# Two token tiles of the last second-layer chunk as float32r matmuls

## The chip, the cores and the metric

The kernel runs on one core of a Trainium2 chip. The metric is the device time of one execution in microseconds. A core has five engines that run side by side and meet by semaphores: TensorE (PE, matmuls; its weight loads are shown apart as PEld), VectorE (DVE), ScalarE (ACT), GpSimd (POOL) and SyncE (SP, which here only starts transfers).

## The reference

```python
# q, k, v: (8, 8, 576, 64) float32; heads 0-3 see the last 32 positions, heads 4-7 every 32nd
scores = where(mask, q @ k.T / 8, -1e9)
attn = softmax(scores)
x = (attn @ v).transpose(0, 2, 1, 3).reshape(4608, 512)
# w_in: (512, 2048), w_out: (2048, 512)
h = x @ w_in
r = maximum(h, 0)
g = r * r
out = g @ w_out                       # (4608, 512) float32
```

It is a sparse attention over 8 batches and 8 heads, followed by two dense layers with a squared ReLU between them, over 4608 tokens.

## The kernel before

Attention writes its result, transposed and in bf16, into four tiles `xt` of 128 channels by 4608 tokens. The dense layers work through nine chunks of 512 tokens. In each chunk the first layer (`mm1`) goes through 16 blocks of 128 hidden units: four matmuls of 512 columns each, from `w_in_b` and `xt`, into one of TensorE's accumulation banks; ScalarE takes the ReLU into a small bf16 tile `r` (four buffers); and one step later (`later(1, ...)`) VectorE multiplies `r` by itself into block `ff` of `g_sb`, a tile of 128 by 16 by 512 in bf16. The second layer (`mm2`) then takes the chunk as four tiles of 128 tokens. For each, 16 matmuls of 512 columns add up over the hidden blocks, with a piece of `g_sb` as the weights and a row of `w_out_b` as the moving operand; ScalarE copies the bank to `y`, and SyncE stores it.

```python
for ff in range(4 * part, 4 * part + 4):
    nc.tensor.matmul(py, g[:, ff, 128 * j:128 * (j + 1)], w_out_b[:, ff, :],
                     start=(ff == 0), stop=(ff == 15))
```

The last tile of the last chunk (`last_y`) is split by columns into 256, 128 and 128, so that its last copy and store are small.

All this stands in one list, `groups`: 288 entries, 16 for the first and 16 for the second layer of each chunk. The last chunk's first layer is entries 256 to 271, its second layer 272 to 287, four entries for each token tile. A hand-written table, `PLAN`, says ahead of which entry each step of attention is issued (loads, transposes, scores, normalisations); the last is at entry 217. Each engine carries out its own instructions in the order in which they are issued (`manual_schedule`), and waits are set where one engine's data is needed by another. So the list and the table set the order.

Memory: most tiles live in the pool `singles` for the whole kernel, and the tiles of attention in this and some further pools (`qk_in`, `qkT`, `v_st`, `rv_pool`, `xl_pool`, `strTq`, `strTk`), all open until the end.

Of the kernel before, what the change touches and what calls it, by code (L numbers as in the profile page):

```python
# [8 lines left out]
FP32 = mybir.dt.float32  # L9
BF16 = mybir.dt.bfloat16  # L10
AF = mybir.ActivationFunctionType
ALU = mybir.AluOpType
# [155 lines left out]
def kernel(  # L168
# [9 lines left out]
    nc = tc.nc  # L178
    B, H, S, D = q.shape
# [6 lines left out]
    NL = S // QL  # L186
# [4 lines left out]
    VP = 72  # L191
    SR = 80
    NP2 = STRIDE // 2
    NG = 5
    NB = NP2 + NG + 1
    W3 = 3 * NA
    RW = STRIDE * D
    ER = S + 32

    singles = ctx.enter_context(tc.tile_pool(name="singles", bufs=1))  # L200
    qk_in = ctx.enter_context(tc.tile_pool(name="qk_in", bufs=4))
    qkT = ctx.enter_context(tc.tile_pool(name="qkT", bufs=4))
    v_st = ctx.enter_context(tc.tile_pool(name="v_st", bufs=1))
    rv_pool = ctx.enter_context(tc.tile_pool(name="rv_pool", bufs=3))
    small = ctx.enter_context(tc.tile_pool(name="small", bufs=4))
    xl_pool = ctx.enter_context(tc.tile_pool(name="xl_pool", bufs=4))
    g_pool = ctx.enter_context(tc.tile_pool(name="g_pool", bufs=2))
    r_pool = ctx.enter_context(tc.tile_pool(name="r_pool", bufs=4))
    y_pool = ctx.enter_context(tc.tile_pool(name="y_pool", bufs=4))

    PS = bass.MemoryType.PSUM
    strTs = {nm: ctx.enter_context(tc.tile_pool(name=f"strT{nm}", bufs=n)) for nm, n in (("q", 2), ("k", 1))}
    psum = ctx.enter_context(tc.tile_pool(name="psum", bufs=1, space=PS))
    psb = psum.tile([128, 8, 512], FP32, name="psb")
    all_banks = [psb[:, i] for i in range(8)]
# [4 lines left out]
    def bank(nm):  # L220
        if places:
            return all_banks[places.pop(0)]
        t = banks[nm].pop(0)
        banks[nm].append(t)
        while id(t) in unread:
            run_due(lambda x: x[1] == unread[id(t)])
        return t
# [10 lines left out]
    NV = 4  # L238
# [1 line left out]
    mask_loc = singles.tile([128, 1, QL], BF16)  # L240
    mask_all = singles.tile([128, NL, QL], BF16)
    mask_str = singles.tile([SP_, 1, SP_], BF16)
    vl_all = singles.tile([128, NV, 2, NL, VP], BF16, name="vl")
    vls = [vl_all[:, i] for i in range(NV)]

    vbds = [singles.tile([128, NB, 128], BF16, name=f"vb{i}") for i in range(2)]
    kbds = [singles.tile([128, NB, 128], BF16, name=f"kb{i}") for i in range(2)]
    ones_bd = singles.tile([128, 128], BF16)
    mask_bd = singles.tile([128, 1, W3], BF16)
    str_rows_t = {nm: singles.tile([SR, RW], BF16, name=f"{nm}_t") for nm in "qk"}  # L250
    kTl = [singles.tile([128, 32 + S], BF16, name=f"kTl{i}") for i in range(NV)]
    es01 = singles.tile([128, 4 * ER], BF16, name="e01")
    es = [es01[:, 0:2 * ER], es01[:, 2 * ER:]] + [singles.tile([128, 2 * ER], BF16, name=f"e{i}") for i in (2, 3)]
    xt = [singles.tile([128, T], BF16, name=f"xt{p}") for p in range(4)]
    w_in_b = singles.tile([128, 4, d_ff], BF16)
    w_out_b = singles.tile([128, 16, d_model], BF16)
# [210 lines left out]
    def later(n, fn, key=None):  # L467
        pending.append((clock[0] + n, key, fn))

    def run_due(test):  # L470
        due = [x for x in pending if test(x)]
        for x in due:
            pending.remove(x)
        for x in sorted(due, key=lambda x: x[0]):
            x[2]()

    def tick():
        clock[0] += 1
        run_due(lambda x: x[0] <= clock[0])
# [247 lines left out]
    gs = {}  # L727
# [3 lines left out]
    def mm1(c, ff, kks=range(4), order=range(4), pool=None):  # L731
        if ff == 0 and c not in gs:
            gs[c] = g_pool.tile([128, 16, 512], BF16, name="g_sb")
        g = gs[c]
        if kks[0] == order[0]:
            phs[ff] = bank(pool or "ph")
        ph = phs[ff]
        for kk in kks:
            nc.tensor.matmul(ph, w_in_b[:, kk, 128 * ff:128 * (ff + 1)],  # L739
                             xt[kk][:, 512 * c:512 * (c + 1)],  # L740
                             start=(kk == order[0]), stop=(kk == order[-1]))
        if kks[-1] != order[-1]:
            return
        r = r_pool.tile([128, 512], BF16, name="r")
        nc.scalar.activation(r, ph, AF.Relu)  # L745
        later(1, lambda: nc.vector.tensor_tensor(g[:, ff, :], r, r, op=ALU.mult))  # L746
# [3 lines left out]
    def mm2(c, i, pool=None):  # L750
        j, part = divmod(i, 4)
        g = gs[c]
        if part == 0:
            if pool == "pt":
                ys[c, j] = bank("pt")
                banks["pt"].remove(ys[c, j])
            else:
                ys[c, j] = bank(pool or "py")
        py = ys[c, j]
# [3 lines that stand above are left out]
        if part == 3:  # L763
            y = y_pool.tile([128, 512], FP32, name="y")
            nc.scalar.copy(y, py)  # L765
            if pool == "pt":
                banks["pt"].insert(0, py)
            r0 = 512 * c + 128 * j
            nc.sync.dma_start(out=out[r0:r0 + 128, :], in_=y)

    NCH = T // 512
# [3 lines left out]
    def last_y(c, j, i):  # L775
        g, r0 = gs[c], 512 * c + 128 * j
        if i == 0:
            ys[c, j] = y_pool.tile([128, 512], FP32, name="y")
        y = ys[c, j]
        cols = (slice(0, 256), slice(0, 256), slice(256, 384), slice(384, 512))[i]  # L780
        ffs = (range(0, 8), range(8, 16), range(16), range(16))[i]
        if i != 1:
            ys[c, j, i] = bank("ph")
        py = ys[c, j, 0 if i == 1 else i]
        for ff in ffs:
            nc.tensor.matmul(py[:, cols], g[:, ff, 128 * j:128 * (j + 1)], w_out_b[:, ff, cols],  # L786
                             start=(ff == 0), stop=(ff == 15))
        if i:
            (V if i == 3 else A)(y[:, cols], py[:, cols])
            (nc.scalar if i == 2 else nc.sync).dma_start(out=out[r0:r0 + 128, cols], in_=y[:, cols])  # L790
# [156 lines left out]
    groups = []  # L947

    def add(c, kind, i, pool=None):
        if kind == 0:  # L950
            groups.append(lambda: None)
        elif kind == 1:
            groups.append(lambda: mm1(c, i, pool=pool))
        elif c == NCH - 1 and i >= 12:
            groups.append(lambda: last_y(c, i // 4, i % 4))
        else:
            groups.append(lambda: mm2(c, i, pool))

    for ff in range(16):
        add(0, 1, ff, {NP: "pt", 8: "py"}.get(ff)) if ff >= NP else add(0, 0, ff)  # L960
    for part in range(4):
        for j, pool in ((0, "ph"), (1, "ph"), (2, None), (3, "pt")):
            add(0, 2, 4 * j + part, pool)
    for i in range(16):
        add(1, 1, i)
# [9 lines left out]
    for line in PLAN.strip().splitlines():  # L975
        n, words = line.split(":")
        plan.setdefault(int(n), []).extend(words.split())
    for n, g in enumerate(groups):
        if n == 32:
            banks["pt"] += banks.pop("py")  # L980
        for word in plan.get(n, ()):
            run_step(word)
        g()
        tick()
# [32 lines left out]
```

## Time and profile before

| | |
|---|---|
| median of two timed runs | 298.03 us (297.99 and 298.07) |
| the profiled execution | 299.14 us |
| its span, first to last instruction | 297.4 us |
| granted TensorE clock | 1.00 |
| PE busy | 287.8 us, 97% of the span |
| DVE busy | 180.3 us, 61% |
| ACT busy | 170.5 us, 57% |
| POOL busy | 73.3 us, 25% |
| first-layer matmuls (L739) on the longest chain | 42% of the span |
| second-layer matmuls (L761) on it | 40% |

The profile is of one execution, whose own time is the 299.14 us; the span leaves out what lies before its first and after its last instruction. Matmuls overlap in the pipeline, so the length recorded for one (379 ns for 512 columns) is more than the distance from one start to the next. A row of a group of instructions gives line, engine, operation, operands, shape and count, then busy time in us and mean length in ns, then the engine's idle time just ahead of them and what ended it. A row of a timeline or of the chain begins with its start and its length in us; several equal instructions in a row are merged there into one with their count.

### The profile page before, as it was taken

To read this page: it belongs to the slowest core of one execution; us is meant where nothing else is said; L and a number is where in the kernel's file an instruction comes from. 1 tells how busy PE (TensorE), PEld (TensorE's weight loads), DVE (VectorE), ACT (ScalarE), POOL (GpSimd) and SP (SyncE) were. 2 spreads that over 40 slices of the span, in tenths; PEclk is the share of its full clock that TensorE was granted. 3 is DMA by queue.
4 is the path that set the end of the run, shared out by engine and by line. 5 is a ranking of instruction groups with operands and counts; after the bars stand their busy time and mean duration, and the time that the engine had idled before them with its cause. 6 is when DMAs were issued, how large, how long until landed. Compare 5 with 4: busy or idle time off the path is not lost.

```text
span 297.4 us, 5621 instructions
## 1 busy us (share of the span) xinstructions
PE 287.8 (97%) x2112; PEld 144.6 (49%) x2148; DVE 180.3 (61%) x465; ACT 170.5 (57%) x318; POOL 73.3 (25%) x107
## 2 busy tenths in 40 slices
PE   7989999999999999999999999999999999999994
PEld 2644555544545454444454445544544444444444
DVE  5557689697777769779367936776575334004300
ACT  3758846774668636764577447744764266127411
POOL 8874743014513036065105700000000000000000
PEclk9999999999999999999999999999999999999999
DMA  7999999999999999999998999411011100020012
GB/s 146 183 207 204 189 199 189 156 224 204 168 179 179 123 164 199 160 144 188 179 128 125 177 149 145 82 55 73 35 31 47 71 37 0 35 89 20 0 71 73
DMA packets 91724, 37.38 MB, mean 126 GB/s; under 512 B 77549, under 2 KB 85831, under 8 KB 91697
## 3 DMA queue, kind: packets, MB, share of 16 engines
q0 software_dynamic: 50608, 18.33, 55.8%
q1 hardware_dynamic: 40944, 18.62, 32.3%
q8 instruction: 17, 0.28, 0.4%
q14 instruction: 11, 0.08, 0.1%
q10 hardware_dynamic: 144, 0.07, 0.1%
HBM read 37.22 MB, written 9.44 MB: 157 GB/s over the span
## 4 chain that ended last, share of the span: by engine, by line
PE 94%; DMA 2%; issue 1%; DVE 1%; ACT 0%; POOL 0%; DVEq 0%; POOLq 0%
PE psb L739 42%; PE psb L761 40%; DMA w_out_b<-in_k_dram 2%; PE psb L699 2%; PE psb L621 1%; PE psb L607 1%; PE psb L786 1%; PE psb L618 1%; PE psb L583 1%; PE psb L538 1%; PE psb L486 1%; DVE xt L668 0%; PE psb L508 0%; PE psb L333 0%; DVE x_l L688 0%
## 5 line engine op out<-in xcount | busy, mean ns | idle before, releaser
L739 PE MATMUL psb<-xt,w_in_b 128*128 128x512 bf16 x558 | 132.1, 379 | 1.2 <-DVE xt L668 0.2
L761 PE MATMUL psb<-w_out_b,g_sb 128*128 128x512 bf16 x542 | 125.3, 379 | 1.2 <-issue 0.5
L745 ACT ACTIVATE r<-psb 128x512 bf16<-128x512 f32 x144 | 85.3, 599 | 37.9 <-PE psb L739 32.8
L746 DVE TENSOR_TENSOR g_sb<-r 128x512 bf16<-128x512 bf16 x144 | 60.4, 423 | 68.5 <-ACT r L745 67.2
L739 PEld LDWEIGHTS <-w_in_b 128*128 128x128 bf16 x576 | 53.2, 97 | 58.9 <-issue 1.4
L761 PEld LDWEIGHTS <-g_sb 128*128 128x128 bf16 x560 | 52.0, 98 | 57.9 <-DVE g_sb L746 0.3
L765 ACT COPY y<-psb 128x512 f32<-128x512 f32 x35 | 20.6, 588 | 51.6 <-PE psb L761 48.6
L631 DVE TENSOR_TENSOR xt<-psb,rv 64x144 bf16<-64x144 f32 x84 | 34.0, 405 | 12.7 <-ACT rv L624 11.6
L623 ACT ACTIVATE rv<-psb 128x432 f32<-128x432 f32 (+1 forms) x21 | 10.5, 501 | 12.8 <-PE psb L618 12.8
L705 DVE TENSOR_TENSOR x_l<-psb,rinv 96x384 bf16<-96x384 f32 x28 | 15.5, 553 | 1.0
L361 POOL DMA_DIRECT2D q_t<-in_q_dram x6 | 3.3, 544 | 45.8 <-DMA qT_s<-q_t 44.9
L594 ACT ACTIVATE e<-psb 128x384 bf16<-128x384 f32 x30 | 12.0, 513 | 4.2 <-PE psb L583 4.2
L608 ACT ACTIVATE e<-psb 128x432 bf16<-128x432 f32 (+1 forms) x21 | 10.4, 496 | 4.0 <-PE psb L607 4.0
L637 DVE TENSOR_TENSOR xt<-psb,rv 64x270 bf16<-64x270 f32 (+1 forms) x28 | 11.0, 433 | 2.5 <-ACT rv L624 2.3
L290 POOL DMA_DIRECT2D q_l<-in_q_dram x16 | 12.0, 754 | 1.6 <-DMA q_l<-in_q_dram 1.4
L290 POOL DMA_DIRECT2D k_l<-in_k_dram x16 | 11.7, 736 | 1.6 <-DMA v_st<-in_v_dram 1.5
L624 ACT ACTIVATE rv<-rv 128x432 f32<-128x432 f32 (+1 forms) x21 | 11.2, 533 | 0.7
L590 DVE TENSOR_TENSOR e<-e,mask_all 128x576 bf16<-128x576 bf16 x20 | 8.4, 456 | 4.9 <-ACT e L594 4.9
L699 PEld LDWEIGHTS <-e 128*128 128x128 bf16 x168 | 8.0, 97 | 4.6
L361 POOL DMA_DIRECT2D k_t<-in_k_dram x6 | 3.2, 536 | 25.0 <-DMA kT_s<-k_t 22.9
L699 PE MATMUL psb<-vl,e 128*128 128x65 bf16 x168 | 9.0, 193 | 0.0
L607 PEld LDWEIGHTS <-kb 128*128 128x128 bf16 x154 | 6.8, 96 | 4.5
(119 smaller groups left out, 213.5 us busy)
## 6 DMA issues: line engine op xcount, KB each, us to landing
out_dram<-y SPq DMA_DIRECT2D x35, 256.0 KB, 4.2
w_out_b<-in_moe_w_out_dram POOLq DMA_DIRECT2D x4, 512.0 KB, 15.1
q_t<-in_q_dram POOLq DMA_DIRECT2D x7, 288.0 KB, 7.3
k_t<-in_k_dram POOLq DMA_DIRECT2D x7, 288.0 KB, 6.9
vl<-in_v_dram POOLq DMA_DIRECT2D x6, 288.0 KB, 7.7
v_st<-in_v_dram POOLq DMA_DIRECT2D x7, 216.0 KB, 6.8
w_in_b<-in_moe_w_in_dram POOLq DMA_DIRECT2D x2, 704.0 KB, 14.3
k_l<-in_k_dram POOLq DMA_DIRECT2D x16, 72.0 KB, 7.0
```

The lines of the kernel that those rows point to most:

```text
L290: nc.gpsimd.dma_start(out=t[:, :, hh, :], in_=src[b, 2 * p + hh].rearrange("(t p) d -> p t d", p=QL))
L594: nc.scalar.activation(e[:, row, 4 * QL * i:4 * QL * (i + 1)], bk[row][i][:, 0:4 * QL], AF.Exp, scale=scale)
L624: nc.scalar.activation(rv, rv, AF.Exp, scale=-1.0)
L631: nc.vector.tensor_tensor(to[:, :, NJ * part:NJ * (part + 1), par], of, by, op=ALU.mult)
L637: nc.vector.tensor_tensor(t, of[:, g:, :, lo:lo + k], by[:, g:, :, lo:lo + k], op=ALU.mult)
L699: nc.tensor.matmul(po[:, n, :], e[:, c:c + 128], rhs[:, NL * part + n, 0:D + 1], start=True, stop=True)
L705: nc.vector.tensor_tensor(x, po[0:QL, :, 0:D], rinv[0:QL].to_broadcast([QL, NL, D]), op=ALU.mult)
L739: nc.tensor.matmul(ph, w_in_b[:, kk, 128 * ff:128 * (ff + 1)], xt[kk][:, 512 * c:512 * (c + 1)], start=(kk == order[0]), stop=(kk == order ...
L745: nc.scalar.activation(r, ph, AF.Relu)
L746: later(1, lambda: nc.vector.tensor_tensor(g[:, ff, :], r, r, op=ALU.mult))
L761: nc.tensor.matmul(py, g[:, ff, 128 * j:128 * (j + 1)], w_out_b[:, ff, :], start=(ff == 0), stop=(ff == 15))
L765: nc.scalar.copy(y, py)
```

## The change

The pools that only attention uses, and the attention tiles out of `singles` (now in `att_singles`), are put on a stack of their own, `att`. Ahead of entry 230, after the last step of attention has been issued, this stack is closed, and a pool `late` is opened in the freed memory. It holds a float32r copy of the whole of `w_out_b`, a small tile of zeros in bf16, and for each of two token tiles a float32r copy of its part of `g_sb`.

- `widen`, ahead of entries 230, 232, ... 244: the first call sets the zeros on VectorE; each of the eight calls has GpSimd copy two of the 16 rows of `w_out_b` (1024 elements per partition) into the float32r tile.
- `mm2_r(0)` at entry 272 and `mm2_r(1)` at entry 276 stand in for token tiles 0 and 1 of the last chunk. Each first makes its float32r copy of g: blocks 0 to 7 by a copy, blocks 8 to 15 by a sum with the zeros, on VectorE for tile 0 and on GpSimd for tile 1. Then tile 0 runs 16 matmuls of 512 columns, and tile 1 runs 16 matmuls for the left 256 columns and 16 for the right, all with float32r operands. ScalarE's copy to `y` and the store follow as before.
- A float32r matmul stands in the order as one instruction that brings its own weights, where a bf16 one is a weight load and a matmul. So TensorE has 48 instructions in place of 64 there; all others, on all engines, keep their order. VectorE has three instructions more, GpSimd ten.

The rest of the last chunk (tiles 2 and 3) and all other chunks stay as they are.

```diff
-    qk_in = ctx.enter_context(tc.tile_pool(name="qk_in", bufs=4))
...
+    att = ctx.enter_context(ExitStack())
+    att_singles = att.enter_context(tc.tile_pool(name="att_singles", bufs=1))
+    qk_in = att.enter_context(tc.tile_pool(name="qk_in", bufs=4))
...
-    vl_all = singles.tile([128, NV, 2, NL, VP], BF16, name="vl")
+    vl_all = att_singles.tile([128, NV, 2, NL, VP], BF16, name="vl")
...
+        elif c == NCH - 1 and i < 8:
+            groups.append((lambda: mm2_r(i // 4)) if i % 4 == 0 else (lambda: None))
...
+    F32R = mybir.dt.float32r
+    wide = {}
+
+    def widen(i):
+        if not wide:
+            att.close()
+            late = ctx.enter_context(tc.tile_pool(name="late", bufs=1))
+            wide["w"] = late.tile([128, 16, 512], F32R, name="w_out_r")
+            wide["z"] = late.tile([128, 8, 128], BF16, name="zeros")
+            nc.vector.memset(wide["z"], 0.0)
+            wide["g"] = [late.tile([128, 16, 128], F32R, name=f"g_r{j}") for j in range(2)]
+        nc.gpsimd.tensor_copy(wide["w"][:, i:i+2, :].rearrange("p a c -> p (a c)"), w_out_b[:, i:i+2, :].rearrange("p a c -> p (a c)"))
+
+    def mm2_r(j):
+        c = NCH - 1
+        r0 = 512 * c + 128 * j
+        y = y_pool.tile([128, 512], FP32, name="y")
+        py = bank("ph")
+        gr, w = wide["g"][j], wide["w"]
+        eng = nc.vector if j == 0 else nc.gpsimd
+        g = gs[c][:, :, 128 * j:128 * (j + 1)]
+        eng.tensor_copy(gr[:, 0:8], g[:, 0:8])
+        eng.tensor_tensor(gr[:, 8:16], g[:, 8:16], wide["z"], op=ALU.add)
+        for lo, hi in ((0, 512),) if j == 0 else ((0, 256), (256, 512)):
+            for ff in range(16):
+                nc.tensor.matmul(py[:, lo:hi], gr[:, ff, :], w[:, ff, lo:hi], start=ff == 0, stop=ff == 15)
+        nc.scalar.copy(y, py)
+        nc.sync.dma_start(out=out[r0:r0 + 128, :], in_=y)
+
     for n, g in enumerate(groups):
+        if 230 <= n < 246 and n % 2 == 0:
+            widen(n - 230)
```

More of the change, by code (lines that the diff above doesn't have):

```diff
@@ L200 @@
     singles = ctx.enter_context(tc.tile_pool(name="singles", bufs=1))
-    qk_in = ctx.enter_context(tc.tile_pool(name="qk_in", bufs=4))
-    qkT = ctx.enter_context(tc.tile_pool(name="qkT", bufs=4))
-    v_st = ctx.enter_context(tc.tile_pool(name="v_st", bufs=1))
-    rv_pool = ctx.enter_context(tc.tile_pool(name="rv_pool", bufs=3))
     small = ctx.enter_context(tc.tile_pool(name="small", bufs=4))
-    xl_pool = ctx.enter_context(tc.tile_pool(name="xl_pool", bufs=4))
     g_pool = ctx.enter_context(tc.tile_pool(name="g_pool", bufs=2))
@@ L209 @@
     y_pool = ctx.enter_context(tc.tile_pool(name="y_pool", bufs=4))
+    att = ctx.enter_context(ExitStack())
+    att_singles = att.enter_context(tc.tile_pool(name="att_singles", bufs=1))
+    qk_in = att.enter_context(tc.tile_pool(name="qk_in", bufs=4))
+    qkT = att.enter_context(tc.tile_pool(name="qkT", bufs=4))
+    v_st = att.enter_context(tc.tile_pool(name="v_st", bufs=1))
+    rv_pool = att.enter_context(tc.tile_pool(name="rv_pool", bufs=3))
+    xl_pool = att.enter_context(tc.tile_pool(name="xl_pool", bufs=4))
     PS = bass.MemoryType.PSUM
-    strTs = {nm: ctx.enter_context(tc.tile_pool(name=f"strT{nm}", bufs=n)) for nm, n in (("q", 2), ("k", 1))}
+    strTs = {nm: att.enter_context(tc.tile_pool(name=f"strT{nm}", bufs=n)) for nm, n in (("q", 2), ("k", 1))}
     psum = ctx.enter_context(tc.tile_pool(name="psum", bufs=1, space=PS))
@@ L242 @@
     mask_str = singles.tile([SP_, 1, SP_], BF16)
-    vl_all = singles.tile([128, NV, 2, NL, VP], BF16, name="vl")
+    vl_all = att_singles.tile([128, NV, 2, NL, VP], BF16, name="vl")
     vls = [vl_all[:, i] for i in range(NV)]
-    vbds = [singles.tile([128, NB, 128], BF16, name=f"vb{i}") for i in range(2)]
-    kbds = [singles.tile([128, NB, 128], BF16, name=f"kb{i}") for i in range(2)]
+    vbds = [att_singles.tile([128, NB, 128], BF16, name=f"vb{i}") for i in range(2)]
+    kbds = [att_singles.tile([128, NB, 128], BF16, name=f"kb{i}") for i in range(2)]
     ones_bd = singles.tile([128, 128], BF16)
     mask_bd = singles.tile([128, 1, W3], BF16)
[L250 to L253, printed above, removed]
+    str_rows_t = {nm: att_singles.tile([SR, RW], BF16, name=f"{nm}_t") for nm in "qk"}
+    kTl = [att_singles.tile([128, 32 + S], BF16, name=f"kTl{i}") for i in range(NV)]
+    es01 = att_singles.tile([128, 4 * ER], BF16, name="e01")
+    es = [es01[:, 0:2 * ER], es01[:, 2 * ER:]] + [att_singles.tile([128, 2 * ER], BF16, name=f"e{i}") for i in (2, 3)]
     xt = [singles.tile([128, T], BF16, name=f"xt{p}") for p in range(4)]
```

## The prediction

> **What bounds the kernel now.** I read the page first, then the chain of waits, then the timeline of the stretch in which the changed tiles run. The page, its lines on the span, the engines' busy time, the clock and the chain:
>
> ```profile
> span 297.4 us, 5621 instructions
> PE 287.8 (97%) x2112; PEld 144.6 (49%) x2148; DVE 180.3 (61%) x465; ACT 170.5 (57%) x318; POOL 73.3 (25%) x107
> PEclk9999999999999999999999999999999999999999
> PE 94%; DMA 2%; issue 1%; DVE 1%; ACT 0%; POOL 0%; DVEq 0%; POOLq 0%
> ```
>
> TensorE is the bound: 97% busy, at full clock in all 40 slices, and 94% of the chain. So a microsecond added to TensorE, or a microsecond in which it has to wait, is a microsecond of the kernel. The changed work lies in the last 18 us. The chain of waits there, in order of time (start, length, what):
>
> ```profile
> 270.44 9.23 PE psb L739 x42
> 279.67 1.51 PE psb L761 x7
> 281.18 0.05 issue
> 281.23 8.80 PE psb L761 x40
> 290.03 3.55 PE psb L786 x48
> 293.57 0.04 DVEq L789
> 293.61 0.04 issue
> 293.65 0.29 DVE y L789
> ```
>
> First-layer matmuls of the last chunk (L739) run to 279.67, and the second layer (L761, then the split last tile, L786) follows without a gap. The only hops are 0.04 to 0.05 us. How that gaplessness comes about shows in the timeline at the seam (start, length, engine, line, operation):
>
> ```profile
> 277.13 2.54 PE L739 MATMUL psb<-xt,w_in_b 128*128 128x512 bf16 x11
> 279.47 0.42 DVE L746 TENSOR_TENSOR g_sb<-r 128x512 bf16<-128x512 bf16 x1 [0.44 <-ACT r L745]
> 279.50 5.34 PE L761 MATMUL psb<-w_out_b,g_sb 128*128 128x512 bf16 x23
> 279.70 0.60 ACT L745 ACTIVATE r<-psb 128x512 bf16<-128x512 f32 x1 [0.27 <-PE psb L739]
> 280.33 0.42 DVE L746 TENSOR_TENSOR g_sb<-r 128x512 bf16<-128x512 bf16 x1 [0.44 <-ACT r L745]
> ```
>
> The second layer starts at 279.50, while the last block of g is finished only at 280.33 + 0.42 = 280.75. That costs nothing now, because the blocks are used in order: the 16th matmul of the tile, the one that reads that block, comes 15 matmuls later. This lead is what the change spends. The pace of the matmuls: 11 of them take 2.54 us with 0.38 of that the last one's own length, so 2.16 / 10 = 0.216 us from start to start at 512 columns. For narrower ones:
>
> ```profile
> 289.86 3.70 PE L786 MATMUL psb<-w_out_b,g_sb 128*128 128x256 bf16 x48
> L786 PE MATMUL psb<-w_out_b,g_sb x48: 218/219/273, 289.9 to 293.3; 128*128 128x128 bf16 x32, 128*128 128x256 bf16 x16
> L786 PEld LDWEIGHTS <-g_sb x48: 97/98/98, 289.6 to 293.3; 128*128 128x128 bf16 x48
> ```
>
> 16 of 256 columns and 32 of 128 start within 3.70 - 0.22 = 3.48 us. Counted in units of 128 columns that is 63 steps, 0.055 us each: 0.055 us at 128 columns, 0.11 at 256. Each brings its own weight load, recorded at 98 ns, yet the pace goes down to 55 ns: bf16 weight loads lie wholly under other matmuls.
>
> **The change, part by part.**
>
> *A. Tile 0 gets a wait in front.* Its 16 matmuls read a float32r copy of g. VectorE makes it in two instructions of 1024 elements per partition: a copy (blocks 0 to 7), then a sum with zeros (blocks 8 to 15). In the built order both stand on VectorE behind all 16 squares of the chunk, although the copy needs only the first eight. So the copy cannot start before 280.75. Its price is not in the trace; the nearest rows (mean ns is the number after the busy time):
>
> ```profile
> L309 DVE CAST k_l<-g_sb 96x768 bf16<-96x768 f32 x1 | 0.6, 557 | 0.1
> L430 DVE COPY vb<-v_st 54x1408 bf16<-54x1408 bf16 x14 | 7.4, 531 | 0.5 <-DMA v_st<-in_v_dram 0.3
> L688 DVE TENSOR_TENSOR x_l<-psb,rinv 96x768 bf16<-96x768 f32 x2 | 1.9, 954 | 0.1
> L705 DVE TENSOR_TENSOR x_l<-psb,rinv 96x384 bf16<-96x384 f32 x28 | 15.5, 553 | 1.0
> ```
>
> Below, the all-bf16 copy, 531 x 1024 / 1408 = 0.39 us. Above, the rate at which a float32 operand is worked through one element at a time: (954 - 553) / 384 = 1.04 ns, so 954 + 256 x 1.04 = 1.22 us. The nearest is the cast L309, the other way round but also between float32 and bf16 in SBUF: twice as fast as 1.04, so 557 + 256 x 0.52 = 0.69 us. I take 0.69. TensorE's first float32r matmul waits for nine semaphores, carried by four extra wait instructions; the others have long been reached, and one of the four stands behind the copy's:
>
> ```profile
> L739 PEldq EVENT_SEMAPHORE  x1: 51/51/51, 113.4 to 113.4; - x1
> ```
>
> So it starts at 280.75 + 0.03 + 0.69 + 0.05 (hop, as in the chain) + 0.05 = 281.57 instead of 279.50: **+2.07 us**, with the ends of the copy +1.8 and +2.6. Behind this wait in TensorE's queue stands all that is left of the kernel, and the stores wait for that; nothing can fill the gap, as tiles 2 and 3, which need no copies, come later in the order.
>
> *B. The second half of tile 0.* The sum is priced at the upper rate, 1.22 us, since both operands and the result pass one by one: done at 281.47 + 1.22 = 282.69. Its first reader is the ninth matmul, 281.57 + 8 x 0.216 = 283.30. **0**, covered by 0.6 us. If a GpSimd instruction held VectorE up there, this cover is gone (a rival, below).
>
> *C. Tile 0's matmuls.* 16 x 0.216 before. The trace has no float32r matmul. Low end: the same pace, 0. High end: the weight load, which is now part of the matmul, no longer slips under the one before: 98 ns each, 16 x 0.098 = +1.6. A 512-column matmul leaves 216 ns to hide a load that fits into 55 in bf16; even with twice the bytes it should. I take **0**.
>
> *D. Tile 1 as 32 matmuls of 256 columns.* 32 x 0.108 = 16 x 0.216, so the split costs nothing by columns. But there are now 32 weight loads instead of 16, and 108 ns to hide each. Low end 0.108; if a load of twice the bytes takes 98 + 55 = 0.153 us and only the next can run ahead, the pace is 0.153; if nothing is hidden, 0.108 + 0.098 = 0.206 (+3.1 us). I take the middle of the first two, 0.130: 32 x 0.022 = **+0.7**.
>
> *E. Tile 1's copies on GpSimd.* The copy waits for the eighth square, the sum for the last. The rows for it:
>
> ```profile
> 273.43 0.43 DVE L746 TENSOR_TENSOR g_sb<-r 128x512 bf16<-128x512 bf16 x1 [0.44 <-ACT r L745]
> ```
>
> ```profile
> 169.59 0.62 POOL L426 DMA_DIRECT2D v_st<-in_v_dram  x1
> ```
>
> ```profile
> L898 POOL MEMSET kb<- 128x1408 f32 x2 | 2.6, 1291 | 0.0
> masks.py:199 POOL TENSOR_SCALAR_AFFINE_SELECT ident<-ident 128x128 bf16<-128x128 bf16 x1 | 0.3, 287 | 0.1
> ```
>
> GpSimd is idle from 170.2 on. 1024 elements cost it between 0.94 us (the memset's 0.917 ns) and 2.3 us (the short select's 2.24 ns, fixed cost included). The copy runs from 273.86 and is done by 276.2. The sum runs from 280.8; even behind both of VectorE's instructions it ends at 282.69 + 2.3 = 285.0. Tile 1 begins at 281.57 + 3.45 = 285.02, and the ninth matmul, the first reader, at 285.9. **0**, covered by 0.9 us.
>
> *F. The eight copies of w_out on GpSimd, and the zeros on VectorE.* 8 x 0.94 to 8 x 2.3 = 7.5 to 18.4 us. They wait for the last users of the freed memory:
>
> ```profile
> 217.88 4.81 SPq L714 DMA_TRANSPOSE xt<-x_l  x2
> 233.04 1.57 DVE L637 TENSOR_TENSOR xt<-psb,rv 64x270 bf16<-64x270 f32 x4 [1.13 <-ACT rv L624]
> 239.76 0.43 DVE L746 TENSOR_TENSOR g_sb<-r 128x512 bf16<-128x512 bf16 x1 [5.14 <-ACT r L745]
> L905 DVE MEMSET xt<- 128x256 uint32 x1 | 0.3, 272 | 0.9 <-PEq L1001 0.9
> ```
>
> All of that is over at 234.6, so they end by 253.0, 28 us ahead of their reader. Nothing stands behind them on GpSimd but tile 1's copies, 20 us later. The zeros take about 2 x 0.27 = 0.54 us among squares that have 0.44 us idle before each, with four r buffers between them and ScalarE: a delay of 0.1 us that the next square makes good. **0** each. The pools that are moved change no instruction's place and no wait before these.
>
> *Sum.* 2.07 + 0 + 0 + 0.7 + 0 + 0 = +2.8 us. The profiled execution, 299.14 us with a span of 297.4, would become 301.9; the median of the two runs, 298.03, lies 1.1 lower, and I forecast there: **300.8 us**.
>
> **The rivals.**
>
> *1. Weight loads in series: slower.* Speaks for it: the load is part of the matmul and has no place of its own in the order, so that it may not be pulled ahead. Against: in bf16 nearly half of a 128-column step's load record lies under other work. Price: 1.6 + 3.1 + 2.07 = +6.8, 304.8 us. With +2.07 from A, it crosses 2% (+5.96) once 48 matmuls lose 81 ns each. Chance 0.14.
>
> *2. A 4-byte stream at half rate: slower.* The weight load is hidden, but each row brings twice the bytes: 0.431 us at 512 columns, 0.216 at 256, so twice 3.45 us more: 2.07 + 6.9 = +9.0, 307.0 us. For it: no 4-byte operand of TensorE is in this trace, so nothing shows that its read has bytes to spare. Against: with 128 columns a weight load and a moving read go on side by side every 55 ns, so in bf16 its reads are not at their end. Chance 0.08. The Trainium skill, SBUF, section "A bandwidth-pool intuition that's wrong (but worth ruling out)", gives TensorE's moving read as about 614 GB/s, written out as 2 bytes per lane and cycle; held to that, this rival would come true. No row here shows it. The skill's FP8 and Floating Point Precision, section "TensorE Precision Notes", speaks the other way: it describes a reduced mode that reads 4-byte values and truncates them, beside a true float32 of four passes.
>
> *3. The change is no reduced mode: four passes, as for float32: slower.* 3 x 6.9 = 20.7 more, +22.8, 320.8 us. Chance 0.05.
>
> *4. The sum on GpSimd goes ahead of VectorE's.* Both become ready while VectorE's copy runs. If GpSimd's gets hold of what they share at 281.47, VectorE's sum ends at 281.47 + 2.3 + 1.22 = 284.99, and the ninth matmul waits 1.7 us: 302.5 us, within 2%. For it: both start within 0.7 us of each other on the same tiles. Against: VectorE's is next in its own queue. Chance 0.06. The skill's SBUF, section "SBUF: two separate sides", calls the port pair of the two engines an exclusive lock that the first one holds for its whole instruction; no instruction of GpSimd that reads SBUF meets VectorE late in this trace, so it cannot say.
>
> *5. Faster.* There is no step that shortens TensorE's work, only 48 issues in place of 64, and issue is 1% of the chain. Chance 0.01.
>
> **How the numbers follow.** The forecast (A with one pass and nearly hidden loads) 0.66, rival 4 0.06, rival 1 0.14, rival 2 0.08, rival 3 0.05, faster 0.01. Slower by over 2%, about what a measurement of this kernel can tell from no change: 0.14 + 0.08 + 0.05 = 0.27; within 2%: 0.72; faster: 0.01. Range: the low end is the short copy and no loss in D, 298.03 + 1.8 = 299.8, less a little for noise; the high end takes in rival 1, 304.9. Left outside: rivals 2 and 3 and 0.03 more.
>
> **What would show it.** In the chain after: a piece of VectorE (the copy) of 0.4 to 1.2 us between the last square and the first float32r matmul, and a gap of about 2.1 us on TensorE between the layers. Starts of tile 0's matmuls 0.216 us apart, of tile 1's 0.108 to 0.153; 0.3 apart is rival 1, 0.43 rival 2, 0.86 rival 3. No wait at the ninth matmul of either tile. The w_out copies over before 253. The forecast is wrong if the gap is under 1.7 or over 2.7 us, or if the two tiles together take over 8.3 us.

## The result and the profile after

The changed kernel takes 302.21 us (median of two runs, 301.97 and 302.44) against 298.03 us before (297.99 and 298.07): a ratio of 1.014, 95% interval 1.0096 to 1.0184. It is 4.2 us slower, by less than 2%. The forecast was 300.8 us.

The profiled execution took 301.97 us. Three of the four lines of its page that were shown of before (the page's own chain breaks off at 283.92, so its shares do not compare):

```profile
span 300.1 us, 5680 instructions
PE 288.9 (96%) x2128; PEld 148.2 (49%) x2164; DVE 184.3 (61%) x468; ACT 170.6 (57%) x318; POOL 84.4 (28%) x117
PEclk9999999999999999999999999999999999999999
```

TensorE's busy time rose by 1.1 us and the span by 2.7, so most of the loss is idle TensorE. The shares can't say where; the timeline of the seam can (start, length, engine, line, operation, and in brackets the idle time before it and what ended it):

```profile
277.25 1.89 PE L741 MATMUL psb<-xt,w_in_b 128*128 128x512 bf16 x8
279.80 0.43 DVE L748 TENSOR_TENSOR g_sb<-r 128x512 bf16<-128x512 bf16 x1 [0.44 <-ACT r L747]
280.14 0.69 DVE L1003 CAST g_r<-g_sb 128x1024 fp32r<-128x1024 bf16 x1
280.31 2.52 POOL L1004 TENSOR_TENSOR g_r<-g_sb,zeros 128x1024 fp32r<-128x1024 bf16 x1 [5.89 <-DVE g_sb L748]
280.75 3.17 DVE L1004 TENSOR_TENSOR g_r<-g_sb,zeros 128x1024 fp32r<-128x1024 bf16 x1
281.04 2.09 PE L1007 MATMUL psb<-w_out_r,g_r 128*128 128x512 f32 x8 [1.90 <-issue]
284.06 5.92 PE L1007 MATMUL psb<-w_out_r,g_r 128*128 128x512 f32 x40 [0.93 <-DVE g_r L1004]
289.82 3.63 PE L763 MATMUL psb<-w_out_b,g_sb 128*128 128x512 bf16 x15
297.07 0.29 DVE L791 COPY y<-psb 128x128 f32<-128x128 f32 x1 [13.16 <-ACT y L791]
```

TensorE now stops twice. The first float32r matmul starts at 281.04. The last first-layer matmul started at 277.25 + 1.89 - 0.38 = 278.76, so without a wait it would have started at 278.98: 2.06 us lost. Eight matmuls later it stops again, until VectorE's sum ends (280.75 + 3.17 = 283.92). That sum is recorded with 3.17 us, because GpSimd's sum for tile 1, ready earlier, ran from 280.31 to 282.83. The chain of waits shows the sum's hop as its "issue" (start, length, what), and behind it a gapless TensorE to the end:

```profile
283.92 0.14 issue
284.06 5.92 PE psb L1007 x40
289.97 0.23 PE psb L763
290.21 0.05 issue
290.26 3.18 PE psb L763 x14
293.44 2.65 PE psb L788 x32
296.10 0.02 issue
296.12 0.28 ACT y L791
296.40 0.67 issue
297.07 0.29 DVE y L791
```

To compare the kernels without what lies before the seam and after the last copy, I take as the *tail* the time from the start of the last first-layer matmul to the end of the last copy of y: 279.29 to 293.94 = 14.65 us before, 278.76 to 297.36 = 18.60 after. That is +3.95 us, which is all that the medians show within their interval (2.9 to 5.5 us). From profile to profile it is only 301.97 - 299.14 = +2.83: in this execution the first layer's last matmul came 0.53 us earlier, and from the end of the last copy to the end of the span it is 2.77 us instead of 3.49. The 3.49 is the odd one: every other profile of this case has 2.75 to 2.78 there. So it is chance that the profiled execution came out at the 301.9 us that the prediction names for it.

The tail divides as follows, by these rows and the starts of the single matmuls:

| term | predicted | measured |
|---|---|---|
| A: wait in front of tile 0 | +2.07 | 281.04 - 278.98 = +2.06 |
| B: wait at the ninth matmul | 0 | 284.06 instead of 282.97 = +1.09 |
| C: tile 0's 16 matmuls | 0 | two halves of 1.93 instead of 1.73 = +0.40 |
| D: tile 1's 32 matmuls | +0.7 | 0.120 instead of 0.108 each = +0.38 |
| E, F: GpSimd's copies, zeros | 0 | 0 |
| sum | +2.8 | +3.93 |

### The profile page after: what moved, and what is told of

The parts are those of the page before. It is cut to its first block, busy times and chain, and to the rows that moved or that the text cites. A ratio compares the mean times of both kernels' runs of the same rounds, so it can differ in the third digit from the quotient of the medians.

```text
span 300.1 us, 5680 instructions
## 1 busy us (share of the span) xinstructions
PE 288.9 (96%) x2128; PEld 148.2 (49%) x2164; DVE 184.3 (61%) x468; ACT 170.6 (57%) x318; POOL 84.4 (28%) x117
## 5 line engine op out<-in xcount | busy, mean ns | idle before, releaser
L763 PE MATMUL psb<-w_out_b,g_sb 128*128 128x512 bf16 x510 | 118.4, 379 | 1.2 <-issue 0.5
L748 DVE TENSOR_TENSOR g_sb<-r 128x512 bf16<-128x512 bf16 x144 | 61.4, 429 | 68.0 <-ACT r L747 66.8
L763 PEld LDWEIGHTS <-g_sb 128*128 128x128 bf16 x528 | 48.7, 97 | 54.0 <-DVE g_sb L748 0.3
L767 ACT COPY y<-psb 128x512 f32<-128x512 f32 x33 | 19.4, 589 | 45.9 <-PE psb L763 42.9
L993 POOL CAST w_out_r<-w_out_b 128x1024 fp32r<-128x1024 bf16 x8 | 7.9, 1039 | 62.3 <-PE psb L623 62.3
L1007 PE MATMUL psb<-w_out_r,g_r 128*128 128x256 f32 (+1 forms) x48 | 8.0, 323 | 2.8 <-issue 1.9
L1003 POOL CAST g_r<-g_sb 128x1024 fp32r<-128x1024 bf16 x1 | 1.0, 1040 | 33.7 <-DVE g_sb L748 33.7
```

What stands on the lines that cost most here:

```text
L1007: nc.tensor.matmul(py[:, lo:hi], gr[:, ff, :], w[:, ff, lo:hi], start=ff == 0, stop=ff == 15)
```

## The experiments

The theory after the result: the loss is two waits on the conversions (3.15 us) and a somewhat slower pace of the float32r matmuls (0.8 us). Rivals: the two sums do not exclude each other and VectorE's is slow by itself; the copies cost time beyond being waited for; the float32r matmuls cost far more or less than the two waits.

The runs, with the ratio to the kernel before on the same chip and the tail of the profiled execution against 14.65 us:

| run | ratio, 95% interval | tail, us |
|---|---|---|
| e1_pool_sum_after | 1.0095 (1.0061 to 1.0128) | +4.36 |
| e2_all_dve | 1.0147 (1.0094 to 1.0199) | +4.35 |
| e3_tile2_first | 1.0012 (0.9985 to 1.0040) | +0.62 |
| e4_copies_bf16_mm | 0.9983 (0.9959 to 1.0008) | +0.05 |
| e5_128cols | 1.0131 (1.0109 to 1.0153) | +3.88 |
| e6_float32 | 1.0694 (1.0668 to 1.0719) | +20.65 |
| e7_fill_gap | 1.0095 (1.0076 to 1.0115) | +2.76 |
| e8_bf16_copies | 1.0062 (1.0048 to 1.0077) | +1.74 |
| e9_again (the changed kernel) | 1.0134 (1.0102 to 1.0167) | +3.96 |
| e10_longer_gap | 1.0189 (1.0165 to 1.0213) | +6.89 |
| e11_early_copy | 1.0036 (1.0017 to 1.0056) | +1.50 |
| e12_reverse | 1.0061 (1.0041 to 1.0081) | +2.34 |

### e1: GpSimd's sum after VectorE's

GpSimd's sum reads zeros of its own, which VectorE writes only behind its own sum; so it cannot go first.

```diff
+            wide["z1"] = late.tile([128, 8, 128], BF16, name="zeros1")
...
-        eng.tensor_tensor(gr[:, 8:16], g[:, 8:16], wide["z"], op=ALU.add)
+        eng.tensor_tensor(gr[:, 8:16], g[:, 8:16], wide["z1" if j else "z"], op=ALU.add)
+        if j == 0:
+            nc.vector.memset(wide["z1"], 0.0)
```

> GpSimd's sum for tile 1 reads a second tile of zeros, which VectorE sets right behind its own sum for tile 0, so the two sums can no longer run at once. Theory (the two sums exclude each other, GpSimd's went first): VectorE's sum is recorded at about 1.2 us instead of 3.17, the ninth float32r matmul of tile 0 waits no more, 1.1 us are gained: 301.1 us. GpSimd's sum, 2.5 us, then ends about 285, before tile 1's ninth matmul needs it. Rival (VectorE's sum into float32r takes 3.2 us by itself): its record stays at 3.2 and the time at 302.2 us or a little above.

Its timeline at the seam:

```profile
281.02 1.22 DVE L1005 TENSOR_TENSOR g_r<-g_sb,zeros 128x1024 fp32r<-128x1024 bf16 x1
281.32 9.34 PE L1010 MATMUL psb<-w_out_r,g_r 128*128 128x512 f32 x48 [1.90 <-issue]
282.87 2.12 POOL L1005 TENSOR_TENSOR g_r<-g_sb,zeros 128x1024 fp32r<-128x1024 bf16 x1 [8.17 <-DVE zeros L1007]
```

VectorE's sum alone takes 1.22 us, the price of the prediction, and the 48 matmuls run without a second wait. The six executions at full clock took 300.94 to 301.74 us, where 301.1 was expected. So the two sums exclude each other, and that was the wait B: in the changed kernel VectorE's sum is 1.95 us longer because it waited for GpSimd's. The Trainium skill, SBUF — State Buffer, section "SBUF: two separate sides", says that the first of the two engines holds the pair of ports for its whole instruction, where VectorE has two inputs from SBUF and GpSimd reads SBUF; 3.17 against 1.22 us agrees.

Yet the 48 matmuls take 9.34 us, longer than the 7.74 that they take at full clock (e7). The windows of this execution (busy time of TensorE, instructions, granted clock, share of the DMAs, GB/s):

```profile
279.00:282.20 3.20, 1.30 (x6) 1.00 0.00 0
282.25:285.60 3.35, 3.35 (x10) 0.50 0.00 0
285.70:289.00 3.30, 3.30 (x25) 1.00 0.20 79
```

For 3.4 us TensorE's clock was granted at half. In the changed kernel's profile the same stretch has 1.00. That was new; it is followed up in e2, e7, e9 and e10.

### e2: both copies and both sums on VectorE

```diff
-        eng = nc.vector if j == 0 else nc.gpsimd
+        eng = nc.vector
```

> Tile 1's copy and sum go to VectorE too, behind tile 0's; GpSimd has nothing left there. Theory of exclusion: as with the sum moved behind, 301.1 us, VectorE's four instructions 0.69, 1.2, 0.69 and 1.2 us long. Rival (the sum is slow by itself): 3.2 us for each sum, tile 1's comes at 288, and its ninth matmul waits about 1.5 us more: 303.7 us.

```profile
282.86 1.22 DVE L1004 TENSOR_TENSOR g_r<-g_sb,zeros 128x1024 fp32r<-128x1024 bf16 x1
284.60 1.22 DVE L1004 TENSOR_TENSOR g_r<-g_sb,zeros 128x1024 fp32r<-128x1024 bf16 x1
```

Both sums take 1.22 us and nothing waits in the middle, as in e1. But five of six executions had a mean clock of 0.994, what one stretch of 3.4 us at half clock makes of it, and these took 302.6 to 305.1 us, against 300.99 in the one at full clock. So e1 and e2 agree on the wait B. What keeps e2's median up is the clock only in part: two of the five lie 1.6 us above the one at full clock, the other three 3.4 to 4.1. One of those three is the profiled execution, 304.35 us; its tail is that of e1, but its last first-layer matmul starts at 280.87 instead of 279.04, and why is not known.

### e3: the bf16 tile 2 first

Tile 2, which needs no copies, runs before tiles 0 and 1, and so covers the wait A (3.45 us of matmuls against 2.06) and the wait B behind it.

```diff
-        elif c == NCH - 1 and i < 8:
-            groups.append((lambda: mm2_r(i // 4)) if i % 4 == 0 else (lambda: None))
+        elif c == NCH - 1 and 4 <= i < 12:
+            groups.append((lambda: mm2_r(i // 4 - 1)) if i % 4 == 0 else (lambda: None))
+        elif c == NCH - 1 and i < 4:
+            groups.append(lambda: mm2(c, i + 8, pool))
```

> The bf16 tile 2 goes first, then the two float32r tiles, then tile 3 as ever. Its 3.45 us of TensorE lie over the copies and sums. Theory (wait in front 2.07, wait in the middle 1.1, the rest is pace): both waits go, what is left is the slower pace and one late first load, 16 x 0.017 + 32 x 0.012 + 0.1 = 0.75 us, 298.8 us. Rival (a float32r matmul after a bf16 one, or the change of type itself, costs more than the pace shows): 299.5 us or more with a gap on TensorE at the change.

```profile
284.19 3.62 PE L763 MATMUL psb<-w_out_b,g_sb 128*128 128x512 bf16 x15
...
285.96 3.15 DVE L1006 TENSOR_TENSOR g_r<-g_sb,zeros 128x1024 fp32r<-128x1024 bf16 x1
287.46 7.85 PE L1009 MATMUL psb<-w_out_r,g_r 128*128 128x512 f32 x48
```

No idle time stands in brackets before the float32r matmuls, though VectorE's sum is again held for 3.15 us. In this execution, of 303.8 us, the clock was at half from 11.5 to 21.7 us and full from there to the end of the tail, so the tail can be compared. It is 0.62 us longer than before: the slower pace alone. So 3.95 - 0.62 = 3.33 us of the loss belong to the waits (and to what a wait does to the pace behind it, see e12).

### e4: copies made, but not read

```diff
-                nc.tensor.matmul(py[:, lo:hi], gr[:, ff, :], w[:, ff, lo:hi], start=ff == 0, stop=ff == 15)
+                nc.tensor.matmul(py[:, lo:hi], g[:, ff, :], w_out_b[:, ff, lo:hi], start=ff == 0, stop=ff == 15)
```

> All copies, sums, zeros and the later pool stay, but the two tiles' matmuls take the bf16 g and w_out again (tile 1 in two halves of 256 columns). Theory (the copies cost only by being waited for): 298.0 us, TensorE without a gap. Rival (GpSimd's copies hold VectorE up and so delay the first layer, or the moved memory costs something): over 298.6 us, with TensorE waiting in chunk 7 or 8.

The conversions cost nothing by being there: the tail is 0.05 us longer, though VectorE's sum takes 3.15 us in this kernel too. They cost only what waits for them.

### e5: tile 1 in pieces of 128 columns

As e3, with 64 matmuls of 128 columns for tile 1, each with its own weight load.

```diff
-        for lo, hi in ((0, 512),) if j == 0 else ((0, 256), (256, 512)):
+        for lo, hi in ((0, 512),) if j == 0 else ((0, 128), (128, 256), (256, 384), (384, 512)):
```

> As the kernel with tile 2 first, but tile 1 as 64 matmuls of 128 columns. The pace tells what the 12 ns are that a float32r matmul of 256 columns loses. Theory (the weight load, recorded at 188 ns and started only when the matmul before it starts, sets the pace of narrow matmuls): still about 0.120 us apart at 128 columns, tile 1 then takes 64 x 0.120 = 7.7 us in place of 3.84, 302.6 us. Rival (a few ns more per matmul, the load hidden): 0.067 us apart, tile 1 takes 4.3 us, 299.2 us. Second rival (narrow float32r falls back to four passes): 0.22 us apart, 14 us, 309 us.

```profile
282.62 11.12 PE L1009 MATMUL psb<-w_out_r,g_r 128*128 128x512 f32 x80
L1009 PEld LDWEIGHTS psb<-w_out_r,g_r 128*128 128x128 f32 x80 | 10.3, 191 | 0.8
```

The narrow matmuls start 0.112 us apart on average: hardly less than the 0.120 at 256 columns, and twice the bf16 0.056. The weight load seems to be the bound: its record is 191 ns against 98 in bf16, and the loads, too, start 0.11 us apart. A rival is that narrow columns stream at half rate. Against it speaks the first of the 64: its successor starts 57 ns later, at 286.533 after 286.476, as in bf16, and only from the second on it is 0.11. No run varied the load alone, so the load as the bound is argued, not shown. At 256 columns the pace is nearly that of bf16, 0.109 us, with 0.011 us on top.

### e6: true float32

As e3, with `F32R = mybir.dt.float32`.

> As the kernel with tile 2 first, but the two tiles' copies and matmuls in float32 in place of float32r. Theory (float32r is a reduced mode of one pass, float32 takes four): 0.86 us apart at 512 columns and 0.43 at 256, 20.7 us more, 319.5 us. Rival (no difference on this chip): 298.8 us.

```profile
L1009 PE MATMUL psb<-w_out_r,g_r 128*128 128x256 f32 x64 | 14.0, 379 | 0.0
L1009 PE MATMUL psb<-w_out_r,g_r 128*128 128x512 f32 x32 | 13.9, 592 | 0.0
```

Each matmul is recorded as two, 0.429 us apart at 512 columns and 0.216 at 256: 0.86 and 0.43 us for a matmul, four times the bf16 pace. That is rival 3's price (20.7 us more), met by float32 and not by float32r. The Trainium skill, FP8 and Floating Point Precision, section "TensorE Precision Notes", gives float32 four passes; the trace agrees in time (0.86 against 0.216 us).

### e7: the first wait filled with matmuls

As e1, with nine bf16 matmuls of 512 columns on old data, into a bank that nobody reads, ahead of tile 0.

```diff
+        if j == 0:
+            for _ in range(9):
+                nc.tensor.matmul(all_banks[6], idle[:, 0:128], idle, start=True, stop=True)
```

> As the kernel in which GpSimd's sum comes after VectorE's, but nine bf16 matmuls of 512 columns on old data, into a bank that nobody reads, fill the wait in front of tile 0. Theory (the idle 2.1 us make TensorE run at half clock for the 3.4 us after, in some executions): TensorE never idles, no execution shows matmuls 0.427 us apart, the runs lie closely together at about 301.0 us, and none at 302.6 to 303.3. Rival (the half clock comes from the float32r matmuls themselves): it still comes in some executions.

```profile
279.64 2.10 PE L1010 MATMUL psb<-xt 128*128 128x512 bf16 x9
281.71 7.74 PE L1013 MATMUL psb<-w_out_r,g_r 128*128 128x512 f32 x48
```

With the wait filled, the clock is 0.999 or 1.0 in all six executions, and the 48 matmuls take 7.74 us. Six executions alone could have missed it by chance, as e1 had it in three of nine. Taken with e10, where a longer wait brings it every time, it is the idle TensorE, not the float32r matmul, that brings the half clock.

### e8: the same waits, all in bf16

As e1, with `F32R = mybir.dt.bfloat16`: copies, sums and matmuls stay, the type goes.

> As the kernel in which GpSimd's sum comes after VectorE's, but w_out's and g's copies and sums are made in bf16, so the matmuls are bf16 ones, 16 of 512 and 32 of 256 columns, behind the same waits. Theory (waits cost 2.07, type only 0.75): VectorE's copy takes 0.4 us in place of 0.69, so the wait in front is 1.8 us, the pace 0.216 and 0.108: 299.8 us, and in some executions half clock after the wait, 1.7 us more. Rival (the cost is that of the type): 298.3 us.

```profile
281.28 0.42 DVE L1004 COPY g_r<-g_sb 128x1024 bf16<-128x1024 bf16 x1
281.61 0.68 DVE L1005 TENSOR_TENSOR g_r<-g_sb,zeros 128x1024 bf16<-128x1024 bf16 x1
281.80 7.11 PE L1010 MATMUL psb<-w_out_r,g_r 128*128 128x512 bf16 x48 [1.53 <-DVE g_r L1004]
```

The tail is 1.74 us longer with no float32r at all: the wait for a copy is most of the cost, and it shrinks with the copy (0.42 us instead of 0.69). I had expected the half clock in some executions; with this shorter gap it came in none of six.

### e9: the changed kernel once more

> The changed kernel unaltered, for more executions. Theory (the wait of 2.07 us brings half clock for 3.4 us in some executions, by where it falls between fixed 3.41 us steps of the clock, seen at 282.21 and 283.53 in two kernels with the same wait): its times fall in two groups, near 302.0 and near 303.7 us, with about two to six in ten in the upper. Rival (the two traces were disturbed by something else): one group near 302.0 to 302.4.

Six executions: 301.83, 301.91 and 302.28 us at a clock of 0.999 to 1.0, 302.82 twice at 0.994, and 305.24 at 0.989, about two such stretches' worth. So the changed kernel, too, seems to get the half clock, in half of its executions; the two runs behind its median had none. One stretch costs 0.9 us here, less than the 1.7 that I expected. A slowed first half of tile 0 would overlap with the wait B; the profiled execution was one at full clock, so neither this nor the place of the stretches is shown.

### e10: a longer wait

As e1, with tile 0's copy made three times, so that TensorE waits 1.45 us longer.

```diff
-        eng.tensor_copy(gr[:, 0:8], g[:, 0:8])
+        for _ in range(1 if j else 3):
+            eng.tensor_copy(gr[:, 0:8], g[:, 0:8])
```

> As the kernel in which GpSimd's sum comes after VectorE's, but VectorE makes tile 0's copy three times, so the wait in front is 1.2 us longer, 3.27 us. Theory of the clock steps: a wait of 3.27 us fills more than half of one 3.41 us step wherever it begins, so half clock follows in every execution or nearly: all near 301.1 + 1.2 + 1.7 = 304.0 us, in one group, and the trace shows 0.427 us between matmuls for 3.4 us. Rival (half clock is chance, whatever the length): two groups, 302.3 and 304.0 us.

```profile
283.17 10.42 PE L1011 MATMUL psb<-w_out_r,g_r 128*128 128x512 f32 x48 [3.36 <-issue]
```

```profile
279.50:282.10 2.60, 0.31 (x2) 1.00 0.00 0
282.15:285.50 3.35, 2.33 (x6) 0.50 0.00 0
285.60:288.90 3.30, 3.30 (x10) 0.50 0.00 0
289.00:292.00 3.00, 3.00 (x25) 1.00 0.23 87
```

All five executions lost clock: 0.994 (one stretch of 3.4 us) or 0.987 (two, as in these windows). So they fall in two groups, 303.6 to 304.4 and 305.0 to 305.6 us, where one near 304.0 was expected. The longer the wait, the surer the half clock.

### e11: tile 0's copy four squares earlier

As e1, with the copy of blocks 0 to 7 issued on VectorE when only they are needed, between the squares.

```diff
+        if n == 268:
+            nc.vector.tensor_copy(wide["g"][0][:, 0:8], gs[NCH - 1][:, 0:8, 0:128])
```

> As the kernel in which GpSimd's sum comes after VectorE's, but VectorE makes tile 0's copy of blocks 0 to 7 four squares before the last. Theory: the first float32r matmul follows the first layer with at most 0.1 us between, and the ninth waits for the sum: last square's end + 1.2 + 0.15 lies 2.6 us behind the seam, eight matmuls take 1.9, so about 0.65 us; with the pace's 0.7 and two late first loads in all 1.5 us over the kernel before, 299.5 us, and no half clock. Rival (the early copy holds back a square that a matmul of the first layer needs in turn): 300 us or more, with a gap in the first layer.

```profile
276.90 0.69 DVE L1019 CAST g_r<-g_sb 128x1024 fp32r<-128x1024 bf16 x1
279.22 2.09 PE L1011 MATMUL psb<-w_out_r,g_r 128*128 128x512 f32 x8
280.48 1.23 DVE L1006 TENSOR_TENSOR g_r<-g_sb,zeros 128x1024 fp32r<-128x1024 bf16 x1
281.85 5.89 PE L1011 MATMUL psb<-w_out_r,g_r 128*128 128x512 f32 x40 [0.54 <-DVE g_r L1006]
```

The wait A is gone: the float32r matmuls start right behind the first layer, and what remains is 0.7 us at the ninth, whose sum needs the last square. So A was the place of the copy on VectorE and nothing else.

### e12: hidden blocks in reverse

As e3, with `for ff in reversed(range(16))`: the first matmul reads the sum, the last half the copy. Meant to tell whether the matmuls are slow by themselves (0.233 us at 512 columns) or by the waits near them.

> As the kernel with tile 2 first, but the float32r matmuls take the hidden blocks from the last to the first, so that the first one waits for the last copy of w_out and the others wait for nothing. Theory (the 17 ns that a float32r matmul of 512 columns loses are its waits): 0.216 us apart, tile 0 takes 3.45 us, 298.5 us. Rival (they are not): still 0.23 us apart, 298.8 us.

```profile
280.84 3.14 DVE L1006 TENSOR_TENSOR g_r<-g_sb,zeros 128x1024 fp32r<-128x1024 bf16 x1
284.19 7.72 PE L1009 MATMUL psb<-w_out_r,g_r 128*128 128x512 f32 x48 [1.51 <-ACT y L767]
```

My number missed: the first matmul now needs the sum that GpSimd holds up to 283.98, beyond the cover of tile 2, so TensorE waits 1.67 us. For the question itself it serves. Behind the first seven matmuls the pace settles at 0.227 us, while in the changed kernel it is 0.224 to 0.236, about 0.233. So of the 17 ns above the bf16 pace at most 6 belong to what waits nearby, and not always: in e9's profile the first half of tile 0 runs at 0.227 right behind the wait A. The 11 that are left, and the 11 at 256 columns, stay unexplained.

## Why the prediction was right or wrong

*What bounds it, and the sign:* right. Every microsecond of wait in front of TensorE was lost, and nothing shortened its work.

*A, +2.07:* right in the mechanism and in the copy's price: 0.69 us, as taken from the rate of the cast between float32 and bf16. That the sum is right to 0.01 us is in part luck: the copy's record starts 0.09 us before the last square's end (280.14 against 280.23) and not 0.03 behind it, and from its end to the first matmul it is 0.21 us (280.83 to 281.04) instead of 0.10. e11 takes the wait away by moving that copy alone, and e3 covers it.

*B, 0:* the step that failed, at +1.09 us; the cover of 0.6 us was worked out for a sum that starts at 281.47 and takes 1.22. The 1.22 was right (e1), the start was not. Rival 4 came, to which I gave 0.06. My argument against it, that VectorE's sum is next in its own queue, does not bear: GpSimd's sum needs only the last square, which ends at 280.23, and starts at 280.31, while VectorE's stands behind its own copy. My own working had it: E lets GpSimd's sum run from 280.8, before the 281.47 of VectorE's. GpSimd's record begins within VectorE's cast and is 0.40 us longer than the 2.12 of e1. Whether it was held until the cast ended, or ran slowly beside it, the rows can't tell; either way it had the port when VectorE's sum came. Rival 4's price of 1.7 took 2.3 + 1.22 = 3.52 us from the copy's end to that of VectorE's sum; it was 283.92 - 280.83 = 3.09, and the slower pace of tile 0 gave the ninth matmul another 0.2 us of cover.

*C, 0, bound +1.6:* under-sized by 0.40. Part of it is the first matmul after each wait: the second follows 0.306 us later, as no weight load has run ahead; the rest is a pace of 0.233 for 0.216.

*D, +0.7:* over-sized by 0.3. The pace was 0.120, between the column rate of 0.108 and my 0.130: a load recorded at 0.19 us lets matmuls follow at 0.120, and e5 finds its limit at 0.11 us. C and D together were forecast at 0.7 and took 0.78, so that here two misses cancel.

*E and F, 0:* right in what they cost.

```profile
231.79 7.93 POOL L993 CAST w_out_r<-w_out_b 128x1024 fp32r<-128x1024 bf16 x8 [62.34 <-PE psb L623]
273.38 1.04 POOL L1003 CAST g_r<-g_sb 128x1024 fp32r<-128x1024 bf16 x1 [33.66 <-DVE g_sb L748]
```

```profile
L748 DVE TENSOR_TENSOR g_sb<-r x6: 425/426/943, 272.0 to 276.3; 128x512 bf16<-128x512 bf16 x6
```

Eight copies of 1.04 us are over at 239.72, near the lower bound. But GpSimd's cast held a square of VectorE (943 ns instead of 425, the longest in the second row), something that E and F do not name. It was harmless there, between squares with 0.44 us of idle time; the same exclusion in B was not.

*Rivals 1 and 2:* fell by the pace: 0.306 appears only behind a wait, and 0.227 to 0.236 is far from 0.43. The figure from the Trainium skill beside rival 2, 2 bytes per lane and cycle for TensorE's moving read, stands there for bf16 and does not carry over to float32r here: 4-byte rows stream at 0.227 us for 512 columns, where it would give 0.431. *Rival 3* is float32, not float32r (e6). *Rival 5:* no run was faster than before beyond its interval; the best float32r order, e3, is level with it, so no version beats both kernels.

*The sum:* forecast +2.8 from the median, measured 3.95 in the tail and 4.2 in the medians; 1.09 of the difference is B. The time lies inside the range, but the range's high end was set for rival 1, which did not come.

*Its own signs:* the gap of 2.06 us lies between 1.7 and 2.7, the copies of w_out are over before 253, and the paces, 0.233 and 0.120, are nearest to those of the forecast. Two signs failed, both by B: there is a wait at the ninth matmul, and the two tiles together take 281.04 to 289.82 = 8.78 us, over the 8.3; without B it would be 7.69.

## What to carry to other kernels

A conversion put at the seam of two layers costs what waits for it, not what it takes: place it where its operands become ready (e11), or run first the tile that doesn't need it (e3). When two engines share a port, ask which instruction becomes ready first, by what each waits for and stands behind; the order within one queue says nothing about the other engine. A wait on TensorE can cost more than its length, since the clock may follow.

## What the hardware showed that was not expected

*A wait of 2 us can halve TensorE's clock.* Behind the wait A of about 2.07 us the granted clock was 0.50 for 3.41 us in the profiles of e1 and e2. By a mean clock of 0.994 or less, which does not show the place, it came in 11 of 23 executions with that wait (e1 three of nine, e2 five of six, e9 three of six, neither of the two first runs of the changed kernel). With 1.7 us (e8, e12) or a filled gap (e7) it came in none of 15, with 3.5 us (e10) in all five. The kernel before shows such a mean clock in 4 of 55 executions, and e3, e4 and e11 in two of 12 each, so something else can bring it too; in e3's profile that stretch lay at 11.5 to 21.7 us. In e1 and e2 the stretch begins 276.48 us after the one in which the clock first rises to full (5.73 to 282.21 us, and 7.05 to 283.53). That is 81 times 3.413 us, the length of the half-clock stretch in e1; in eight of the other profiles the clock falls near the span's end, 293.55 us after its rise, 86 times as much. So the clock changes on a grid of fixed steps. In e1's, from 278.80 to 282.21, TensorE idled some 2.07 / 3.41 = 60%. In those of the changed kernel's profile and of e8 it idled 50 to 54% at most, which left the clock alone. So what would decide is where the wait falls in the grid; a threshold between 54 and 60% is an estimate from these few profiles. For the way back it would be another: in e10 TensorE idled only from 282.12 to 283.17, 31%, of the first half-clock stretch, and the second followed. The Trainium skill, TensorE: Matmul & The Clock Gate, section "HAM oscillation — how this bites in real kernels", warns of idle gaps over about 3.4 us, and section "What's actually happening" of a free-running window of 3413 ns; the grid agrees, the length of the gap does not: 2.07 us was enough.

*float32r streams at nearly the bf16 rate down to 256 columns.* 0.227 to 0.236 us at 512 columns and 0.120 at 256, against 0.216 and 0.109 in bf16; at 128 it is 0.112 against 0.056, where the weight load seems to set it.

*GpSimd holds up a VectorE instruction with two inputs, whether it has two itself or one.* A sum on VectorE went from 1.22 to 3.17 us behind a sum on GpSimd, and a square from 0.43 to 0.94 us beside a one-input cast there. The other direction is open: GpSimd's sum took 2.49 to 2.52 us in the seven profiles in which its record begins within VectorE's cast, and 2.12 to 2.14 in the five in which it stands alone, which fits a wait as well as a slower run.
